# Attention and a softplus FFN on one core: the order tables of tiles 1 to 8, with GpSimd's block sums gathered between its maxima

## The chip, the cores and the metric

One core of a Trainium2 chip runs the whole program. The metric is device microseconds of one execution, as the median of 3 runs.

## The reference, cut to what matters

```python
q_s = softmax(q, axis=-1)            # max, exp, sum + 1e-9, divide; 64 values each
k_s = softmax(k, axis=2)             # over the 576 positions of a head
kv  = einsum('bhsd,bhse->bhde', k_s, v)
x   = einsum('bhsd,bhde->bhse', q_s, kv)   # 8 batches, 8 heads, 576 positions, 64 wide
x   = x.transpose(0, 2, 1, 3).reshape(4608, 512)
h   = x @ w_in                        # 512 x 2048
g   = maximum(h, 0) + log1p(exp(-abs(h)))
out = g @ w_out                       # 2048 x 512, float32
```

## The kernel before

The 4608 tokens are cut into 9 tiles of 512 (`SUBS`). The hidden width 2048 is cut into 16 chunks of 128. Float32 matrices are split into a high and a low part, so that one product costs three matmuls of 128x512. For each tile and chunk there is an up product (12 matmuls into a `ph` bank), ScalarE's softplus, a split into `g_hi` (ScalarE, L772) and `g_lo` (VectorE, L773), and two chunks later a down product (12 matmuls into the `po` banks).

Stage A is tile 0, ordered by the table `FIRST`. Stage B is tiles 1 and 2, ordered by `SINGLE`: 32 lines, one for each chunk. Line n says which steps are issued at three places, between bars: behind the up product of chunk n, behind its softplus, and behind the down product of chunk n-2. Within a line the split of chunk n-1 comes behind the first part. Stage C is tiles 3 to 8 in three pairs, ordered by the three lists of `PAIRS`. It uses fewer up products by working on sums and differences of `w_in` blocks and of token blocks. An engine executes its own instructions in the order in which they are issued, so these tables are the schedule; there is no planner at run time.

The steps in `SINGLE` prepare the next tiles. The first digit is the tile.

- `2u30` to `2u35` belong to one pair of heads of batch 2 (head pair 3): `0` the maximum of k over positions within a partition (VectorE, L418) and then across partitions (GpSimd's `partition_all_reduce`, L420, tile `mb`); `2` the subtraction of `mb` (VectorE, L435); `3` the exponential (ScalarE, L443); `4` the reciprocal of the sums (VectorE); `5` the split into `kv_hi` and `kv_lo` (ScalarE and VectorE in turn, L477 to L479). `2u3*` is the place at which the TensorE products of that unit stand (L448).
- `2q0` to `2q11` are the softmax of q: maxima of the two halves (`0`, `1`), exchange (`2`), subtraction (`3`, `4`, L573), exponential (`5`, `6`), sums (`7`, `8`, L579), inversion (`9`) and division (`10`, `11`).
- `2x00` to `2x33` are the product of q and kv: transposition (L661), split (L666, L668), TensorE's product at `2x0*` (L674), addition, and for tile 2 one more split.
- `p3` writes the w_in and w_out parts of chunk pair 3 to DRAM for stage C. `s30` to `s33` compute the sums of that pair's w_in blocks, mostly on GpSimd: `0` two additions (L974), `1` four additions of 128x256 (L977 to L980), `2` a copy on ScalarE (L984) and a subtraction on GpSimd (L985), `3` the stores by DMA (L990, L991).
- `f0` to `f10` prepare the sums of x for a pair, `U` and `D` load w for stage C, `2Q0` loads half a tile of q.

The sums need a place in SBUF, which is that of another tile that is dead by then; `SUM_SLOTS` lists them.

Of the kernel before, what the change touches and what calls it, by code (L numbers as in the profile page):

```python
# [44 lines left out]
SINGLE = [
    "||2u00",
    "2q0 2q1 2q2 2u10|p1 2u02 h0 2q4 2u12|",
    "2q6 s00 2q3 2u03 2u13|h1|2u0* 2u1* s01",
    "p0|2u14 2u20 2q5 2q8 2u22|2u30 2u04",
    "2u15||2u05",  # L50
    "s02 2u32 2u33 2u23 2q7 2q9 2q10|s10|2u2* 2d1 2u3*",
    "2u24 2u25 2x00 2d0|2u34 2x01 s11 2u35 3u00|",
    "2x0*|2x02 s12|s03",
    "2x03 2d2 s13 2x10 2x11||2q11 2x1* 2Q0 2x12 2d3 2x13",
    "2x20|2x21|",
    "2x2*||2x22 3u02",
    "2x23 2x30 3q0 2x31||3u10 2x3* 2x32 p2 3u12",
    "|2Q1 3q1|3u13 3q2",
    "p3 3q3 2x33 3q4 3u03 3u0* 3u1*|3u14 3u20 3u04 3q5 3q6|",
    "3u15|3q8 3u30 3u22 3u05 3q7 3u32|",  # L60
    "|3u23|3q9",
    "3u33|3u2* 3u3* 3q10 3u24|3u34 3u25",
    "3x00 3u35 3x01 4u00|4u10|3x0*",
    "s20 3x02 3x10 s21||p4 3x11 3q11",
    "s22 3x1* 3x12||3x20 3x21",
    "s23 s40||3x2*",
    "3x22|3x30 4u12 s41 s30|3Q0 p5",
    "3x31 s31 4u02 3Q1 s42|3x3* 4u13|",
    "4q0 3x32 s50 4q1 s43 4u03 s51 4u0* f0 4q2 s32|4u1* 4q3|4q4 s52 4u14",
    "s33 4u20|4q6 4u15 4q5|",  # L70
    "4u04 4u22 p7 s60 s53 4u30|p6 4u05 4u32 4q8 4q7 f1 4u33 s61 s70 4u23|",
    "||4q9 4u2* 4u3* 4u24 4q10 4u34 4u25 U0 U1 4x00 4u35 4x01 s71 4q11 s72",
    "||",
    "4x0* 4x02 4x10|4x11 s62|",
    "4x1* 4x12 s63 4x20||s73 4x21 f2",
    "4x2* 4x22 4x30|4x31|f4",
    "|4x3* 4Q1|4Q0 U2 4x32 D0 D1 D2",
]
PAIRS = [
    [  # L80
        "f5 f3 f6|S1.0 J1.0",
        "|f7 f10 S2.0",
        "f8 au00 f9 S3.0 J3.0|aq0 L1.0",
        "L4.0|au10 aq1 J2.0 g1.0",
        "|S1.1 au02 J1.1 aq2 au03",
        "g4.0 S2.1 au0* L1.1 aq3|L3.0 au12 au13",
        "aq4 S3.1|au04 J3.1",
        "aq6 aq8 J2.1 L4.1|",
        "g1.1|aq5 g4.1 S1.2 J1.2 au1*",
        "L2.0 S2.2 au20|",  # L90
        "au05 au14 S3.2 J3.2 aq7|",
        "au22 au30|au15 L1.2 L4.2 J2.2 g1.2",
        "au32 au23 S1.3|aq9 J1.3 au33 aq10",
        "g4.2 au2* au3* au34 au24 aq11 L1.3|L3.1 S2.3",
        "|au25 S3.3 J3.3 au35 ax00 g1.3 ax01",
        "bu00 L4.3|ax0* J2.3 ax02 ax10",
        "|aQ0 S1.4 J1.4 ax11",
        "ax1*|S2.4 g4.3",
        "L1.4 S3.4 bu10 bu12 J3.4 bq0|ax12 ax20 g1.4",
        "|L4.4 J2.4 ax21 L2.4",  # L100
        "S1.5 L2.1 ax2* J1.5|g4.4 bu02",
        "L1.5|L3.2 ax22 ax30 S2.5 ax31 aQ1 L3.4",
        "S3.5 J3.5|",
        "|g1.5 J2.5 bq1 L4.5 L2.2 bu03 bu13 bq2",
        "S1.6|ax3* J1.6 bq3",
        "ax32 bu0* bq4 bq5 S2.6 bq6 g4.5 L1.6 bu1*|bu14 L3.3",
        "S3.6 J3.6|bu04 L2.3 bq7",
        "J2.6 bu20 g1.6 L4.6|",
        "|bu30 S1.7 J1.7",
        "bq8 bu22 bu05 bu15 g4.6 bu32 S2.7|L1.7 bu23",  # L110
        "S3.7 bu33|bu2* L3.5 J3.7 bq9 bu3*",
        "|bu24 g1.7 bu25 L4.7 bq11 bq10 bu34 bx00 L2.5 J2.7 L2.6 g4.7",
        "bu35 bx01|",
        "G0|bx0*",
        "|",
        "G1 L2.7 bx02|G2 L3.6 bx10",
        "bx11|",
        "bx1* G3 G4|bQ0",
        "bx12 bx20|G5 bx21 L3.7",
        "|nf0 G6 bx2* nf1",  # L120
        "G7|nf2",
        "|bx22 bx30 G8",
        "|bx31 G9",
        "bx3* G10 bx32|",
        "|G11",
        "bQ1 nf4|nf10",
        "G12|",
        "nf5 G13 nf6 nf8|G14 nf3 nf9 G15 nf7",
    ],
    [  # L130
        "S1.0 J1.0|",
        "|S2.0 au00 L1.0",
        "au02 S3.0 au10|au12 J3.0",
        "L4.0|J2.0",
        "g1.0 aq1|S1.1 g4.0 J1.1 au13",
        "|S2.1 L3.0",
        "|aq0 S3.1 L1.1 au03 J3.1",
        "au0* au1*|J2.1 au04 aq2 L4.1 g1.1",
        "au14 au15 S1.2 aq4|J1.2 au05",
        "aq3 S2.2 L1.2|",  # L140
        "g4.1|aq5 au20 au30 S3.2 aq6 au22 J3.2",
        "aq7 au32 g1.2 J2.2|L4.2 au23",
        "S1.3 J1.3|g4.2",
        "S2.3 aq8 au33|",
        "au2* au3* au24|S3.3 L3.1 L3.2 J3.3 aq9 aq10 au34 L1.3 au25",
        "J2.3 ax00|L4.3 au35",
        "g1.3 ax01 S1.4 J1.4|ax0* ax02 g4.3 ax10",
        "bu00 S2.4|ax11 aq11 L1.4",
        "bu10|aQ0 S3.4 J3.4 L2.1 bu12 bu02 ax1* ax12",
        "L4.4|L2.3 J2.4",  # L150
        "ax20 g1.4 ax21 S1.5 bu13|J1.5 g4.4 ax2*",
        "L1.5|bq0 ax22 ax30 S2.5",
        "ax31 L2.4 S3.5|J3.5 bu03 g1.5 aQ1 L2.0 ax3* ax32 L3.5 bq1",
        "bu0*|J2.5 bu1* bq2 L4.5",
        "|bu20 bu04 bq4 bu22 bu30 g4.5 bu23 S1.6 bu14 bq6 J1.6",
        "L2.5 S2.6|L2.2",
        "S3.6 bu15 L3.3|J3.6 L1.6",
        "J2.6 bu32 L4.6 g1.6 bq3|",
        "L2.6|bq8 bu05 L3.4 S1.7 J1.7 g4.6",
        "|bq5 bu2* bq7 bu33 bq9 S2.7 bu3* bu34",  # L160
        "|bu24 bq10 bu25 bx00 S3.7 L1.7 bu35 J3.7",
        "g1.7 L4.7 bq11 J2.7|L3.7",
        "|bx01 g4.7",
        "bx0* G0 bx02|bx10",
        "|G1 G2",
        "|bx11",
        "G3 nf0|bx1*",
        "|G4",
        "bx12 G5|",
        "bx20 bx21 G6|",  # L170
        "bx2*|",
        "G7 bx22 bQ0|G8 bx30",
        "|nf2 L3.6",
        "bx31 G9 G10 bx3* nf4|",
        "bx32|G11",
# [7 lines left out]
        "L1.0 S3.0|J3.0",
        "g1.0 L4.0 J2.0|",
        "S1.1 g4.0 J1.1|",
        "L1.1 S2.1|L2.0",
        "|S3.1 J3.1",
        "|L4.1 g1.1 J2.1",
        "L3.0 S1.2 J1.2|g4.1",
        "|S2.2 L1.2",  # L190
        "S3.2 J3.2|",
        "J2.2 L4.2|L2.2 g1.2",
        "|S1.3 J1.3",
        "g4.2 S2.3 L1.3|",
        "S3.3 J3.3|g1.3",
        "L4.3 L2.1|J2.3",
        "S1.4 g4.3 L3.3 J1.4|",
        "|S2.4",
        "L3.2 L1.4|S3.4 J3.4",
        "|J2.4 L4.4",  # L200
        "g1.4|S1.5 J1.5 g4.4",
        "S2.5|",
        "S3.5|J3.5",
        "L1.5 J2.5|L4.5 g1.5",
        "S1.6 L3.1|L2.5 J1.6 L1.6 L3.4",
        "|g4.5 S2.6",
        "S3.6|J3.6",
        "|g1.6 L4.6 J2.6",
        "S1.7 J1.7|",
        "|S2.7 g4.6",  # L210
        "L1.7 L2.4 S3.7|J3.7",
        "|g1.7 J2.7 L4.7",
        "g4.7|",
        "G0 L3.6|",
        "|G1 L2.7 L2.6 L3.5 G2",
# [7 lines left out]
        "G8 G9|",
        "|G10",
        "G11|",
        "|G12",
        "|G13",
        "G14|",
# [1044 lines left out]
```

## Time and profile before

| | us |
|---|---|
| median of 3 runs | 892.82 (892.55 to 892.94) |
| the profiled execution | 891.69 |
| its span, first to last instruction | 889.9 |
| TensorE (PE) busy | 833.5 |
| VectorE (DVE) busy | 549.3 |
| ScalarE (ACT) busy | 520.4 |
| GpSimd (POOL) busy | 114.0 |

The span is covered by stage A from 0 to 119.67 us, stage B to 365.30 us and stage C to the end; the boundaries are the first up product of tile 1 and the first matmul of line 1118. Busy time of TensorE includes matmuls at half speed. A wait in brackets in a row names what ended it; "issue" means that the profile shows nothing that ended it. MODIFY_POOL_CONFIG is an instruction of GpSimd's sequencer, which the program's order shows as a bare "ISA" row.

### The profile page before, as it was taken

Reading aid. Unit: us, or ns where it says so; the run is one execution under the profiler, and the core shown is the slowest. Engines: PE = TensorE matmul, PEld = TensorE weight load, DVE = VectorE, ACT = ScalarE, POOL = GpSimd, SP = SyncE. Lnnn points to the kernel's source line nnn. Section 1 sums busy time; section 2 is a strip of 40 time slices with the busy share of each in tenths; the row PEclk is TensorE's granted clock in tenths of the full one; section 3 lists DMA queues with packets and bytes.
Section 4 is the critical chain, followed back from the end, with each engine's and each line's share of the span. In section 5 each row is a group of like instructions: output and inputs, shape, how many; then the busy total and the mean of one; then the engine's idle time right before and its main releaser. Section 6 shows DMA issues by size and latency. Waiting matters only on the chain.

```text
span 889.9 us, 11526 instructions
## 1 busy us (share of the span) xinstructions
PE 833.5 (94%) x4172; PEld 678.3 (76%) x4172; DVE 549.3 (62%) x849; ACT 520.4 (58%) x863; POOL 114.0 (13%) x203
## 2 busy tenths in 40 slices
...
PEclk9999999889989968999999999999999999999999
...
GB/s 341 376 346 54 26 149 141 101 140 174 78 171 198 275 117 114 277 203 211 233 232 231 245 215 201 218 247 179 202 211 236 190 177 244 164 218 156 142 222 108
DMA packets 79896, 172.72 MB, mean 194 GB/s; under 512 B 5088, under 2 KB 51936, under 8 KB 70624
## 3 DMA queue, kind: packets, MB, share of 16 engines
...
## 4 chain that ended last, share of the span: by engine, by line
PE 73%; DVE 8%; ACT 7%; issue 6%; POOL 3%; DMA 2%; SPq 0%; POOLq 0%; DVEq 0%; ACTq 0%
PE po L1138 28%; PE ph L1118 24%; PE po L795 3%; PE po L793 3%; PE po L794 3%; PE ph L758 3%; PE ph L760 3%; PE ph L759 3%; PE att L674 2%; PE att L448 1%; DMA kvt<-in_kv_tail 1%; DVE g_lo L773 1%; ACT g_hi L772 1%; POOL w L974 1%; PE po L791 1%
## 5 line engine op out<-in xcount | busy, mean ns | idle before, releaser
L1138 PE MATMUL po<-w,g_hi 128*128 128x512 f32 x784 | 246.0, 390 | 0.0
L1118 PE MATMUL ph<-w,w 128*128 128x512 f32 x864 | 213.0, 391 | 1.9 <-ACT w L1189 1.7
L1118 PEld LDWEIGHTS ph<-w,w 128*128 128x128 f32 x864 | 161.4, 188 | 36.8 <-ACT w L1189 2.1
L1138 PEld LDWEIGHTS po<-w,g_hi 128*128 128x128 f32 x784 | 146.8, 188 | 30.3
L1138 PE MATMUL po<-w,g_lo 128*128 128x512 f32 x392 | 153.1, 391 | 0.1
L1192 DVE TENSOR_TENSOR w<-ph,w 128x512 f32<-128x512 f32 x55 | 37.9, 689 | 99.1 <-PE ph L1118 54.5
L773 DVE TENSOR_TENSOR g_lo<-w,g_hi 128x512 fp32r<-128x512 f32 x74 | 51.0, 689 | 56.4 <-ACT g_hi L772 51.7
L1138 PEld LDWEIGHTS po<-w,g_lo 128*128 128x128 f32 x392 | 73.6, 188 | 15.8 <-DVE g_lo L773 0.5
L793 PE MATMUL po<-w,g_hi 128*128 128x512 f32 x164 | 68.5, 418 | 12.1 <-ACT g_hi L772 12.1
L772 ACT CAST g_hi<-w 128x512 fp32r<-128x512 f32 x74 | 45.8, 619 | 55.5 <-PE po L1138 55.1
L795 PE MATMUL po<-w,g_lo 128*128 128x512 f32 x164 | 68.3, 416 | 4.7 <-DVE g_lo L773 4.6
L1189 ACT COPY w<-ph 128x512 f32<-128x512 f32 x55 | 32.1, 584 | 67.2 <-PE ph L1118 67.0
L794 PE MATMUL po<-w,g_hi 128*128 128x512 f32 x164 | 67.7, 413 | 0.0
L420 POOL PARTITION_ALL_REDUCE mb<-mx x28 | 25.4, 906 | 270.7 <-DVE mx L418 231.1
L758 PE MATMUL ph<-x,w 128*128 128x512 f32 x142 | 58.0, 408 | 0.0
L759 PE MATMUL ph<-x,w 128*128 128x512 f32 x142 | 56.3, 397 | 0.0
L760 PE MATMUL ph<-x,w 128*128 128x512 f32 x142 | 56.0, 394 | 0.0
L668 DVE TENSOR_TENSOR two<-att,two 64x512 fp32r<-64x512 f32 x56 | 38.6, 689 | 20.1 <-ACT two L666 19.6
L793 PEld LDWEIGHTS po<-w,g_hi 128*128 128x128 f32 x164 | 32.9, 200 | 19.7 <-ACT g_hi L772 13.2
L773 DVE TENSOR_TENSOR g_lo<-l,g_hi 128x512 fp32r<-128x512 f32 x46 | 37.8, 822 | 11.6 <-ACT g_hi L772 11.0
L666 ACT CAST two<-att 64x512 fp32r<-64x512 f32 x56 | 32.5, 580 | 19.9 <-DVE att L661 19.2
L795 PEld LDWEIGHTS po<-w,g_lo 128*128 128x128 f32 x164 | 33.0, 201 | 14.6 <-DVE g_lo L773 7.4
...
## 6 DMA issues: line engine op xcount, KB each, us to landing
...
```

The costliest lines, as they stand in the source:

```text
L668: nc.vector.tensor_tensor(out=w[SIDE[1 - z], z], in0=ps[zs], in1=w[zs, z].bitcast(F32), op=ALU.subtract)
L758: nc.tensor.matmul(ph, lhsT=w_hi, rhs=x_hi, start=h == 0, stop=False)
L759: nc.tensor.matmul(ph, lhsT=w_lo, rhs=x_hi, start=False, stop=False)
L760: nc.tensor.matmul(ph, lhsT=w_hi, rhs=x_lo, start=False, stop=h == HP - 1)
L772: copy(g_hi, l)
L773: nc.vector.tensor_tensor(out=g_lo, in0=l, in1=g_hi.bitcast(F32), op=ALU.subtract)
L793: nc.tensor.matmul(po, lhsT=g_hi[:, ms], rhs=w_hi, start=j == chunks(t)[0], stop=False)
L794: nc.tensor.matmul(po, lhsT=g_hi[:, ms], rhs=w_lo, start=False, stop=False)
L795: nc.tensor.matmul(po, lhsT=g_lo[:, ms], rhs=w_hi, start=False, stop=j == chunks(t)[-1])
L1118: nc.tensor.matmul(bank, lhsT=a, rhs=b, start=start and e == k == 0, stop=e == 1 and k == 2, skip_group_check=True)
L1138: nc.tensor.matmul(po, lhsT=g[:, cs], rhs=w, start=first and k == 0, stop=end and k == 2)
L1192: nc.vector.tensor_tensor(out=l[k, p], in0=ph_b, in1=l[k, p], op=ALU.add)
```

## The change

The contents of `SINGLE` and `PAIRS` are written anew, with the same steps, and `SUM_SLOTS` gives other places for six of the eight sums. `FIRST` and all functions are as before.

```diff
 SINGLE = [
-    "||2u00",
-    "2q0 2q1 2q2 2u10|p1 2u02 h0 2q4 2u12|",
...
-    "4q0 3x32 s50 4q1 s43 4u03 s51 4u0* f0 4q2 s32|4u1* 4q3|4q4 s52 4u14",
+    "|2u00 2q1 2u10 2u02|",
+    "|2u12 2u03 p1 2q0 2q2 h0 2u13 2q4|",
...
+    "s42 3x21|3x2*|s32 3x22 3x30 s43 s52 3Q1 3x31",
+    "4q1||",
+    "3x3* 4u00|3x32 4u10 p5 4u02|4u12 4u03",
+    "4u13 4u0* 4q0|4u1*|",
+    "s53 p6 4q2 4u04 4q3 4q4 4u20 4u14 4u30 4u22 4q5 4q6|4u32 s33 s60 4u05 4q7 4u33|4q8 4u15 4u23 4q9",
+    "||4u2* 4u24 4u3* 4q10 4u34 U0 4u25",
...
-SUM_SLOTS = "x2", "w1", "x1", "x1", "w3", "w4", "w5", "w6"
+SUM_SLOTS = "x2", "w1", "x0", "x1", "spare", "w2", "w3", "w4"
```

On GpSimd the kernel before has, around the units 0 and 1 of batch 4 (`mb` is the result of the maxima, the `w_` names are parts and sums of w_in, and a bare ISA is MODIFY_POOL_CONFIG):

```order
L985 TENSOR_TENSOR w_2488<-w_2488 128x1024
L420 ISA
L420 ISA mb<-mx 128x128
L974 ISA
L974 TENSOR_TENSOR w_2639<-w_1002 128x512
L974 TENSOR_TENSOR w_2639<-w_1098 128x512
L420 ISA
L420 ISA mb<-mx 128x128
L977 ISA
L977 TENSOR_TENSOR w_2639<-w_2639 128x256
L978 TENSOR_TENSOR w_2639<-w_2639 128x256
L979 TENSOR_TENSOR w_2639<-w_2639 128x256
```

At the same units the changed kernel has (`x_2289`, `spare` and `w_2321` are the sums of the pairs 3, 4 and 5):

```order
L979 TENSOR_TENSOR w_2321<-w_2321 128x256
L980 TENSOR_TENSOR w_2321<-w_2321 128x256
L985 TENSOR_TENSOR spare<-spare 128x1024
L985 TENSOR_TENSOR x_2289<-x_2289 128x1024
L985 TENSOR_TENSOR w_2321<-w_2321 128x1024
L420 ISA
L420 ISA mb<-mx 128x128 x2
L371 MEMSET kvt 64x2x64
```

The two maxima stand behind one another, with one bare ISA row ahead of them instead of one ahead of each and one ahead of each sum. In tiles 1 and 2 and up to the first maximum of stage C there are 12 such rows before and 6 after.

On VectorE the kernel before has, in line 25 of `SINGLE` (tile 4's q and k, two lines into its softmax), between two splits of g:

```order
L773 TENSOR_TENSOR g_lo_1959<-l_1877,g_hi_1958 128x512
L458 TENSOR_SCALAR r_1964<-att1_108 128x1
L459 RECIPROCAL r_1964<-r_1964 128x1
L418 TENSOR_REDUCE mx_1967<-kvt_1936 128x128
L458 TENSOR_SCALAR r_1971<-att0_107 128x1
L459 RECIPROCAL r_1971<-r_1971 128x1
L479 SCALAR_TENSOR_TENSOR kv_hi11_96<-att1_108,r_1964,kv_hi11_96 64x64
L479 SCALAR_TENSOR_TENSOR kv_lo11_104<-att1_108,r_1964,kv_lo11_104 64x64
L773 TENSOR_TENSOR g_lo_2007<-l_1962,g_hi_2006 128x512
```

At the same units the changed kernel has between two splits of g:

```order
L773 TENSOR_TENSOR g_lo_1972<-l_1879,g_hi_1971 128x512
L573 TENSOR_TENSOR q0_1846<-q0_1846,m_1872 128x1024
L479 SCALAR_TENSOR_TENSOR kv_hi11_96<-att1_108,r_1956,kv_hi11_96 64x64
L479 SCALAR_TENSOR_TENSOR kv_lo11_104<-att1_108,r_1956,kv_lo11_104 64x64
L418 TENSOR_REDUCE mx_1997<-kvt_1934 128x128
L418 TENSOR_REDUCE mx_2002<-kvt_1950 128x128
L435 TENSOR_TENSOR kvt_1950<-kvt_1950,mb_2004 128x10x64
L773 TENSOR_TENSOR g_lo_2020<-l_1975,g_hi_2019 128x512
```

A subtraction of q, both maxima of units 2 and 3 and the subtraction of unit 2 now stand ahead of that split; before there was one maximum.

## Rows read from the trace of the kernel before

**Rows 1.** The page: busy time of each engine; TensorE's granted clock in 40 slices.

```profile
PE 833.5 (94%) x4172; PEld 678.3 (76%) x4172; DVE 549.3 (62%) x849; ACT 520.4 (58%) x863; POOL 114.0 (13%) x203
...
PEclk9999999889989968999999999999999999999999
```

**Rows 2.** Busy time by window, stages B and C: length, engines, clock, DMA.

```profile
119.67:365.30 245.63, 208.14 (x1057) 167.42 (x1056) 159.59 (x239) 138.94 (x233) 88.73 (x120) 0.91 0.46 153
365.31:890.00 524.69, 516.36 (x2481) 424.38 (x2479) 281.63 (x426) 283.11 (x467) 14.88 (x42) 1.00 0.59 207
```

**Rows 3.** TensorE's timeline in stage B: start, duration, line, operands.

```profile
119.67 0.39 PE L758 MATMUL ph<-x,spare 128*128 128x512 f32 x1
...
125.11 0.39 PE L758 MATMUL ph<-x,w 128*128 128x512 f32 x1
...
175.49 0.30 PE L674 MATMUL att<-two,kv_hi 128*128 128x128 f32 x1 [2.52 <-DVE two L668]
...
178.20 0.63 PE L794 MATMUL po<-w,g_hi 128*128 128x512 f32 x1
178.63 0.63 PE L795 MATMUL po<-w,g_lo 128*128 128x512 f32 x1
...
188.32 0.22 PE L674 MATMUL att<-two,kv_hi 128*128 128x128 f32 x1
...
188.89 0.39 PE L758 MATMUL ph<-x,w 128*128 128x512 f32 x1
...
282.61 1.39 PE L448 MATMUL att<-kvt 128*64 128x65 f32 x40
```

**Rows 4.** What TensorE waited for, 120 to 366 us: total, times, longest.

```profile
PE att L448 <- issue: 16.1, 2, 13.8
PE po L793 <- ACT g_hi L772: 12.1, 3, 4.6
PE po L795 <- DVE g_lo L773: 4.6, 3, 1.8
```

**Rows 5.** The chain of work that ended last, 296 to 345 us.

```profile
298.88 4.04 issue
...
303.73 7.38 issue
...
313.82 5.81 issue
...
320.44 6.64 issue
```

**Rows 6.** GpSimd's sequencer at line 420, 191 to 210 us: durations (ns), starts.

```profile
L420 POOLq MODIFY_POOL_CONFIG  x2: 4/4/4, 193.0 to 193.0; - x2
```

**Rows 7.** GpSimd's timeline in stage B.

```profile
207.20 0.72 POOL L420 PARTITION_ALL_REDUCE mb<-mx  x1 [14.40 <-DVE mx L418]
...
311.11 2.47 POOL L974 TENSOR_TENSOR w<-w 128x512 f32<-128x512 f32 x2 [7.46 <-issue]
...
339.40 2.36 POOL L985 TENSOR_TENSOR w<-w 128x1024 fp32r<-128x1024 f32 x1 [1.16 <-ACT w L984]
```

**Rows 8.** VectorE's timeline in stage B.

```profile
339.88 2.43 DVE L773 TENSOR_TENSOR g_lo<-l,g_hi 128x512 fp32r<-128x512 f32 x1 [3.57 <-ACT g_hi L772]
...
344.54 0.69 DVE L773 TENSOR_TENSOR g_lo<-l,g_hi 128x512 fp32r<-128x512 f32 x1
```

**Rows 9.** VectorE by line and form, 119.67 to 365.3 us: busy, mean ns, idle before.

```profile
L773 DVE TENSOR_TENSOR g_lo<-l,g_hi 128x512 fp32r<-128x512 f32 x32 | 28.1, 880 | 10.1 <-ACT g_hi L772 9.8
L418 DVE TENSOR_REDUCE mx<-kvt 128x128 f32<-128x640 f32 x12 | 15.8, 1315 | 5.9 <-DMA kvt<-in_kv_tail 4.6 <-POOL x L978 1.2
L435 DVE TENSOR_TENSOR kvt<-kvt,mb 128x640 f32<-128x640 f32 x12 | 10.3, 858 | 24.0 <-POOL mb L420 23.9
L573 DVE TENSOR_TENSOR q<-q,m 128x1024 f32<-128x1024 f32 x6 | 10.0, 1675 | 0.0
L579 DVE TENSOR_REDUCE s<-q 128x32 f32<-128x1024 f32 x6 | 7.2, 1208 | 0.0
```

More of the change, by code (lines that the diff above doesn't have):

```diff
@@ L45 @@
 SINGLE = [
-    "||2u00",
-    "2q0 2q1 2q2 2u10|p1 2u02 h0 2q4 2u12|",
[L48 to L68, printed above, removed]
-    "4q0 3x32 s50 4q1 s43 4u03 s51 4u0* f0 4q2 s32|4u1* 4q3|4q4 s52 4u14",
-    "s33 4u20|4q6 4u15 4q5|",
-    "4u04 4u22 p7 s60 s53 4u30|p6 4u05 4u32 4q8 4q7 f1 4u33 s61 s70 4u23|",
-    "||4q9 4u2* 4u3* 4u24 4q10 4u34 4u25 U0 U1 4x00 4u35 4x01 s71 4q11 s72",
@@ L73 @@
-    "||",
[L74 to L77, printed above, removed]
+    "|2u00 2q1 2u10 2u02|",
+    "|2u12 2u03 p1 2q0 2q2 h0 2u13 2q4|",
+    "2u0* 2q6 2q3 2q8 2u1*|h1|2u20",
+    "|2u04 2u30 2u14 2u05 2u15|",
+    "s00 p0 2u22 2u32||2q5 2u33",
+    "2q7 2q9 2u23|2u2* 2d0 2u24 2u3* 2q10|2u25 2x00",
+    "|s01 2q11|2d1 2u34 2x01 2u35 s02",
+    "s03 2d2 2x0* 2x02||2x03 2d3 2x10 2x11 s10",
+    "||2x1*",
+    "2x12|s11 2x13 s12 p3|s13",
@@ new lines @@
+    "2x20 2x21 2x2* 2x22|2x23|2x30",
+    "3u00 3u10 2x31||3u12 2Q0",
+    "2Q1 3u02 2x3* 2x32 3q1||2x33",
+    "3q0 3q2 p2 3u03 3u13 3u0* 3u1* 3u14 3q4 3u04 p4|3q3 3u15|3q5 3u20 3q6 3u30 3u32",
+    "||",
+    "3q8 3q7 s20 3u22|3u05 3q9 3u33 3q10 3u23|",
+    "3u2* 3u24 3u3*||",
+    "3u25 s21 3u34 3x00 3x01|s22 3q11|",
+    "3u35|3x0* s23 3x02 3x10|3x11 3Q0",
+    "s30 s40 s31||3x1* s50 p7 3x12",
+    "3x20 s41||s51",
+    "s42 3x21|3x2*|s32 3x22 3x30 s43 s52 3Q1 3x31",
+    "4q1||",
+    "3x3* 4u00|3x32 4u10 p5 4u02|4u12 4u03",
@@ L78 @@
+    "4u13 4u0* 4q0|4u1*|",
+    "s53 p6 4q2 4u04 4q3 4q4 4u20 4u14 4u30 4u22 4q5 4q6|4u32 s33 s60 4u05 4q7 4u33|4q8 4u15 4u23 4q9",
+    "||4u2* 4u24 4u3* 4q10 4u34 U0 4u25",
+    "4x00|4u35|4x01",
+    "4x0* f1 4x02 s70 4x10|s71|",
+    "U1 4x11 s72 4q11 4x1* 4x12 4x20||4x21 s61 f0",
+    "4x2*||s73 4x22 4x30 s62",
+    "s63 4x31|U2 D1 4x3*|4Q0 4Q1 f2 4x32 D0 D2 f4",
 ]
@@ L80 @@
     [
[L81 to L114, printed above, removed]
-        "|",
[L116 to L128, printed above, removed]
-    ],
-    [
[L131 to L175, printed above, removed]
-        "|",
-        "L2.7 nf1 G12|nf3 nf5 G13 nf7 nf6 nf8 bQ1 G14",
-        "nf10|nf9 G15",
@@ new lines @@
+        "f5 f3 f6 S1.0 J1.0|",
+        "|f8 f7 f10 S2.0",
+        "au00 f9 S3.0|J3.0",
+        "au02 L1.0 J2.0 au10 L4.0 g1.0|aq1 au12",
+        "|au03 S1.1 J1.1",
+        "|S2.1 au13",
+        "L1.1 aq0 au0* aq2 aq4 S3.1 g4.0 au1*|J3.1",
+        "|g1.1 aq6 L4.1 L3.0 au14 J2.1",
+        "aq3|g4.1 S1.2 J1.2 aq5 au20",
+        "|S2.2 L1.2",
+        "au30|au22 S3.2 J3.2",
+        "aq7|aq8 au15 aq9 J2.2 L4.2",
+        "au04 L3.1 au32 g1.2 g4.2 S1.3 au05 J1.3|",
+        "au23 aq10 au2* S2.3 au33 au3* aq11 au24 au34|L1.3 au25 L2.1",
@@ new lines @@
+        "S3.3 ax00 J3.3|",
+        "ax01 au35 g1.3|J2.3 L4.3 ax0* bu00",
+        "ax02 S1.4 ax10|J1.4",
+        "|L1.4 aQ0 g4.3 ax11 S2.4 ax1*",
+        "ax12|S3.4 J3.4 ax20 g1.4",
+        "J2.4 bq0 ax21 L4.4|bu10",
+        "S1.5 J1.5|ax2* L2.0 ax22",
+        "L2.2 ax30 g4.4 S2.5 bu02|aQ1",
+        "|ax31 S3.5 J3.5 L1.5 ax3* L2.4",
+        "bu12 bq1 bq2 bu13 J2.5 L4.5|g1.5 L3.4 bq4 ax32",
+        "bu03|S1.6 bu0* g4.5 J1.6 bu1*",
+        "bq6|S2.6",
+        "bu20 L2.3 bq3 L3.2 bu04|S3.6 L1.6 bu14 J3.6",
@@ new lines @@
+        "J2.6|L4.6 g1.6",
+        "bq8 S1.7 bu22 bu30|bu23 J1.7 bu32 bq5",
+        "|S2.7 bq7 g4.6 bq9",
+        "bu05 bu15 bu33|bu2* S3.7 bu24 J3.7 bq10 bu3*",
+        "L1.7 g1.7 bu25 bq11 L3.7 bx00 L4.7 bu34 J2.7|L2.5",
+        "g4.7 bx01|G0 bu35",
+        "|G1",
+        "bx0*|bx02",
+        "G2 bx10 L3.6|",
+        "nf1|bx11 L3.3 G3 bx1*",
+        "G4 nf0|",
+        "bx12 bx20 G5|",
+        "bx21|bx2*",
+        "nf2 L2.6 L2.7 G6 G7 bx22 L3.5|G8 bx30 bx31",
+        "|",
+        "G9|",
```

144 lines of the change are left out of this document (99 added, 45 removed).

## The prediction, made before the change was run

> **What bounds the kernel now.** First the page's busy times and its row of the granted clock [rows 1]: TensorE is busy for 94% of the span, and the clock falls below 9 tenths in one region only, the slices from about 155 to 356 us. That region is stage B. The windows by stage say the same in numbers [rows 2]: in stage B TensorE is busy for 208.14 of 245.63 us at a mean granted clock of 0.91; in stage C for 516.36 of 524.69 at 1.00. So idle time is 37.5 us in B and 8.3 in C.
>
> How much of B is loss? A line of the table is 24 matmuls, and at full clock one takes 125.11 - 119.67 = 5.44 us [rows 3]. 32 lines are 174.1 us. Twelve kv units come in six pairs of 1.39 us (8.3), and twelve x products take 188.89 - 188.32 = 0.57 each (6.8) [rows 3]. Together 189.2 us, against 245.6: 56.4 us are lost in B, 37.5 of them idle. Most of the other 19 are matmuls at half speed: behind the gap of 2.52 us they start every 0.43 us (178.20, 178.63) instead of 0.227 [rows 3], which is 1.2 instead of 2.4 GHz.
>
> What TensorE waits for is read next [rows 4]: 16.1 us for kv products (one wait of 13.8), 12.1 for g_hi, 4.6 for g_lo. None of these is slow work. The chain names the cause [rows 5]: between 298 and 328 us it holds four pieces of "issue", 4.04, 7.38, 5.81 and 6.64, which lie alternately ahead of a maximum and ahead of a sum on GpSimd. Each time GpSimd goes from sums to `partition_all_reduce` or back there is a MODIFY_POOL_CONFIG, and then 6 to 7.5 us in which it does nothing [rows 6, 7]: 7.46 from the maximum of 303.6 to the addition of 311.11. VectorE stands at the subtraction of `mb` meanwhile, 23.9 us in all [rows 9], and it issues in order: g_lo and the kv splits behind it are late too.
>
> One more reading decides what a switch costs elsewhere. Before the maximum at 207.20 GpSimd had been idle for 14.40 us, yet it started as soon as VectorE's maximum was there [rows 7]; the switch had begun at 193.0, right behind the last sum [rows 6]. A switch therefore runs ahead of its data, and it is free if about 7 us lie between the last operation of one kind and the first need of the other.
>
> By the Trainium skill (GPSIMD Engine Reference, Instruction dispatch) the first call into freshly loaded code pays about 6 us. The trace agrees for the maxima and shows up to 1.5 us more for the sums.
>
> **The change part by part.** *Switches.* 12 become 6. I went through the six that stay.
> - Lines 4, 15 and 25, into sums (`s00`, `s20`, `s60`): the maxima of all four units are done, so only ScalarE's copies `s02`, `s22`, `s62` need the result, and these stand two to five lines later. 7.5 us and two additions (2.47) and four small ones (3 us) are 13; two lines are 11 us, and for `s22` the switch can start behind the maximum in line 13. No cost.
> - Line 11, into maxima (`3u00`): `s12` is in line 9. No cost; the same for the first maximum of stage C.
> - Line 23, into maxima (`4u00`): three subtractions of 2.4 us stand in lines 21 and 22, then 6 us. By this count the result is there when line 23 is 6 us old, about when VectorE reaches `4u02`. With what VectorE has ahead of it, `4u0*` waits about 1 us.
>
> So the issue pieces of the chain go (the four of [rows 5] are 23.9 us), and with them the backlog that each left on VectorE and ScalarE. What is late next is VectorE's own load.
>
> *Dense lines.* I summed the work by line. Ahead of the exponential `4u23` line 25 has two L573 of 1.68, two maxima of 1.32, two L435 of 0.86, two L579 of 1.21 [rows 9], together 10.1 us, one g_lo of 0.69, and some 20 short operations that I estimate at 3.8: 14.6 us, and about 1.4 for turns with ScalarE. VectorE begins it some 2.4 us ahead of TensorE's line, so `4u23` is through 13.6 us into the line; TensorE arrives at `4u2*` after two lines, 10.9 us. That is a new wait of 2.7 us. Lines 13 to 15 are alike (VectorE 11.0, 0.7 and 7.6 us against 6.8, 5.4 and 5.4), and the same count gives 2.6 us at `3u2*`. Lines 5, 8 and 23/24 give 0.5, 0.5 and 1.0. Sum 7.3 us. Two of these waits are long enough to bring the half clock, as the wait of 2.52 us did [rows 3]; 12 matmuls (one down product) at 0.2 us extra make 2.4 each, 4.8 together. So far 12.1.
>
> *GpSimd beside VectorE.* g_lo took 2.43 us while a subtraction ran on GpSimd (339.40 to 341.76) and 0.69 alone [rows 7, 8]. Eight such subtractions stay. From below the burst costs nothing (lines 19, 20 and 22 have only 2 us of VectorE each); from above each holds one g_lo that TensorE waits for, 8 times 1.74, 14 us. I take half, 7 us, since in the kernel before, too, only some of the slow ones show as waits (4.6 us for g_lo [rows 4]).
>
> The Trainium skill (SBUF — State Buffer, Summary: rules for kernel authors) says that of a VectorE operation with two SBUF inputs and a GpSimd operation the second to issue fully blocks. The trace agrees at 339.88. By the rule alone the burst would hold every such operation in lines 19 to 23; the rival C below prices it.
>
> *Stage C.* Its tables are new as well, with the same steps and the same matmuls. Its idle time is 8.3 us [rows 2], and part of that is the end, which no table moves. So it can hardly gain more than 4 us; `f2` and `f4` now stand at the end of B, which puts about 1 us ahead of the first pair. I take 0, with 4 us gained and 6 lost as ends. *SUM_SLOTS:* each new place is free when it is asked for (the latest is `w2`, free behind the down product of line 19, where `s50` stands); it costs nothing unless the stores come later than in line 18 (`3x02` waits for those of `s23`, hidden by about one line).
>
> Sum: B loses 12 + 7 = 19 instead of 56.4, a gain of 37.4. The profiled execution of 891.69 becomes 854.3; the median is 1.1 above that execution, so 855.4, which I round to 855.
>
> **The rivals.**
> A. The dense lines cost their whole overhang. Lines 13, 15, 25 and 29 have 4.2, 2.1, 9.7 and 2.4 us more VectorE than TensorE; if nothing catches up, 18.4 us and four stretches at half speed (9.6), with 7 for the port and 2 elsewhere make 37 lost, a gain of 19: 873. For it: VectorE is at 15 us in one line of 5.4. Against it: the next lines are nearly empty, and lines of 10 us stood in the table before without waits of their own.
> B. Only the four pieces on the chain go, 23.9 us, and other waits take the place of the backlog: 891.7 - 23.9 + 1.1 = 869. For it: the chain holds them whole. Against it: half the loss of B is neither of them, but the half clock and the late splits that follow.
> C. The burst blocks VectorE. If all eight subtractions hold up TensorE and three of the gaps bring the half clock, 14 + 7 instead of 7: 869. For it: 339.88. Against it: VectorE has little to do there.
> D. Slower. Stage C's new order makes TensorE wait: 96 places in the two pairs that carry attention, and from 0.4 us for each of them (38 us) the gain is gone; at 0.5, 48 us, the time is 903. For it: every row there changed. Against it: there the work on VectorE and ScalarE is 54% of the length each, and TensorE's whole idle time is 8.3 us [rows 2].
> E. The switches are fewer but were hidden anyway: no change. Against it stands the wait of 13.8 us directly behind them [rows 4, 5].
>
> **How the numbers follow.** Forecast 0.60, 843 to 866; A 0.14; B 0.09; C 0.07; D 0.06; E 0.04. The range of 8 in 10 takes in A, B and C, and below it the case that B loses 4 us only and stage C gains 3: 892.8 - 52 - 3 = 838. I give 839 to 881. About 0.2% is what the measurement tells from no change. Faster is the first four, 0.90; within 0.2% 0.04; slower 0.06.
>
> **What would show it.** Right: 6 switches in stage B; no "issue" ahead of the subtraction L435 and no wait of more than 3 us at kv products; the window of B near 208 us with a granted clock of 0.96 or more; C within 5 us of 524.7. The first waits to look for are at `3u2*` and `4u2*`, under 3 us each, with VectorE busy through them. Wrong: a MODIFY_POOL_CONFIG on the chain again, matmuls at half speed over more than two stretches, or C longer by over 10 us.

## The result, and the profile after

The changed kernel takes 854.23 us (median of 4 runs, 853.95 to 854.53), the kernel before on the same chip 892.72; the ratio is 0.957, with a 95% interval of 0.955 to 0.959. The forecast was 855.0. The profiled execution took 854.46 us, with a span of 852.7.

The page of the changed kernel, busy time of each engine and TensorE's granted clock in 40 slices:

```profile
PE 823.4 (97%) x4172; PEld 673.4 (79%) x4172; DVE 543.0 (64%) x849; ACT 519.1 (61%) x861; POOL 115.8 (14%) x203
...
PEclk9999999999999999999999999999999999999999
```

The slices in which the clock lay below 9 tenths [rows 1] are gone. TensorE's busy time fell by 10.1 us with the same 4172 matmuls: fewer of them ran at half speed.

The windows of the changed kernel, stages B and C: length, busy time of PE, PEld, DVE, ACT and POOL, granted clock, DMA share, GB/s:

```profile
119.61:328.55 208.94, 196.87 (x1057) 160.69 (x1056) 152.28 (x239) 136.53 (x231) 88.20 (x120) 0.98 0.53 173
328.56:852.70 524.14, 516.44 (x2481) 424.33 (x2479) 282.92 (x427) 284.35 (x467) 17.15 (x42) 1.00 0.59 209
```

Beside [rows 2], stage B is 36.7 us shorter and stage C 0.6. In B, TensorE's idle time went from 37.5 to 12.1 us and its busy time from 208.1 to 196.9. GpSimd's busy time in B did not change (88.7 and 88.2): its work is the same, and what went are its pauses.

What TensorE waited for in stage B (total, times, longest), and VectorE's wait for `mb`:

```profile
PE att L674 <- DVE two L668: 5.0, 5, 1.9
PE att L448 <- issue: 3.0, 1, 3.0
PE att L674 <- DVE kv_lo L479: 1.7, 2, 1.0
PE att L448 <- ACT kvt L443: 1.2, 2, 1.0
PE att L448 <- POOL x L974: 1.1, 1, 1.1
```

```profile
DVE kvt L435 <- POOL mb L420: 2.0, 3, 0.8
```

Of [rows 4], the wait of 13.8 us is gone, as are the 12.1 for `g_hi` and the 4.6 for `g_lo`. The subtraction of `mb` waited 23.9 us before [rows 9] and waits 2.0 now.

GpSimd's sequencer from 119 to 366 us, with two rows for each switch (times in ns, then first and last start):

```profile
L420 POOLq MODIFY_POOL_CONFIG  x6: 12/18/28, 187.2 to 324.1; - x6
L974 POOLq MODIFY_POOL_CONFIG  x6: 87/88/88, 145.2 to 286.8; - x6
```

and four places of GpSimd's own timeline:

```profile
194.21 0.73 POOL L420 PARTITION_ALL_REDUCE mb<-mx  x1 [7.21 <-DVE mx L418]
...
222.66 2.50 POOL L974 TENSOR_TENSOR x<-w 128x512 f32<-128x512 f32 x2 [6.91 <-DVE kv_lo L479]
...
270.28 0.72 POOL L420 PARTITION_ALL_REDUCE mb<-mx  x1 [6.74 <-issue]
...
294.42 3.70 POOL L974 TENSOR_TENSOR w<-w 128x512 f32<-128x512 f32 x2 [7.58 <-DVE s L584]
```

Three switches toward each side, 6 instead of 12. The first maximum waited for VectorE's `mx`, not for its switch, which had begun at 187.2. Only at 270.28 (line 23) does the profile name nothing that ended the pause, and TensorE's gap behind it, at `4u1*`, is 0.28 us. The pauses ahead of the two sums are as long as a switch as well, whatever the profile names there, but the sums are for stage C, and TensorE waits for none of them here. The 1.1 us that the list above puts on a sum end at 224.57, when ScalarE's exponential for that product has just ended (224.47). In the kernel before, eight pauses of GpSimd in stage B are put down to "issue", 53.1 us in all; here it is this one.

### The profile page after: what moved, and what is told of

Its sections match the earlier page's. It is cut to its first block, busy times and chain, and to the rows that moved or that the text cites. A ratio compares the mean times of both kernels' runs of the same rounds, so it can differ in the third digit from the quotient of the medians.

```text
span 852.7 us, 11505 instructions
## 1 busy us (share of the span) xinstructions
PE 823.4 (97%) x4172; PEld 673.4 (79%) x4172; DVE 543.0 (64%) x849; ACT 519.1 (61%) x861; POOL 115.8 (14%) x203
## 4 chain that ended last, share of the span: by engine, by line
PE 75%; DVE 9%; ACT 7%; issue 4%; DMA 3%; POOL 2%; SPq 0%; DVEq 0%; ACTq 0%; POOLq 0%
PE po L1138 29%; PE ph L1118 24%; PE ph L758 3%; PE ph L759 3%; PE ph L760 3%; PE po L793 3%; PE po L795 3%; PE po L794 3%; DMA kvt<-in_kv_tail 2%; PE att L674 2%; PE att L448 1%; DVE q L587 1%; DVE g_lo L773 1%; DVE two L668 1%; ACT two L666 1%
## 5 line engine op out<-in xcount | busy, mean ns | idle before, releaser
L1138 PE MATMUL po<-w,g_hi 128*128 128x512 f32 x784 | 246.0, 390 | 0.0
L1138 PEld LDWEIGHTS po<-w,g_hi 128*128 128x128 f32 x784 | 146.7, 188 | 30.4
L1138 PE MATMUL po<-w,g_lo 128*128 128x512 f32 x392 | 152.8, 390 | 0.5 <-DVE g_lo L773 0.5
L773 DVE TENSOR_TENSOR g_lo<-w,g_hi 128x512 fp32r<-128x512 f32 x77 | 52.8, 690 | 56.3 <-ACT g_hi L772 52.5
L1138 PEld LDWEIGHTS po<-w,g_lo 128*128 128x128 f32 x392 | 73.6, 188 | 16.3 <-DVE g_lo L773 0.9
L793 PE MATMUL po<-w,g_hi 128*128 128x512 f32 x164 | 65.3, 398 | 0.0
L795 PE MATMUL po<-w,g_lo 128*128 128x512 f32 x164 | 64.9, 396 | 0.0
L794 PE MATMUL po<-w,g_hi 128*128 128x512 f32 x164 | 64.9, 396 | 0.0
L420 POOL PARTITION_ALL_REDUCE mb<-mx x28 | 28.1, 1003 | 256.5 <-DVE mx L418 236.8
L758 PE MATMUL ph<-x,w 128*128 128x512 f32 x142 | 56.9, 400 | 0.0
L759 PE MATMUL ph<-x,w 128*128 128x512 f32 x142 | 55.5, 391 | 0.0
L760 PE MATMUL ph<-x,w 128*128 128x512 f32 x142 | 55.4, 390 | 0.0
L418 DVE TENSOR_REDUCE mx<-kvt 128x128 f32<-128x640 f32 x28 | 36.9, 1329 | 9.9 <-DMA kvt<-in_kv_tail 9.8
L766 ACT ACTIVATE l<-ph 128x512 f32<-128x512 f32 (+1 forms) x50 | 29.1, 581 | 14.9 <-PE ph L760 13.6
L773 DVE TENSOR_TENSOR g_lo<-l,g_hi 128x512 fp32r<-128x512 f32 x46 | 34.1, 741 | 4.8 <-ACT g_hi L772 4.0
```

The costliest lines, as they stand in the source:

```text
L758: nc.tensor.matmul(ph, lhsT=w_hi, rhs=x_hi, start=h == 0, stop=False)
L759: nc.tensor.matmul(ph, lhsT=w_lo, rhs=x_hi, start=False, stop=False)
L760: nc.tensor.matmul(ph, lhsT=w_hi, rhs=x_lo, start=False, stop=h == HP - 1)
L773: nc.vector.tensor_tensor(out=g_lo, in0=l, in1=g_hi.bitcast(F32), op=ALU.subtract)
L793: nc.tensor.matmul(po, lhsT=g_hi[:, ms], rhs=w_hi, start=j == chunks(t)[0], stop=False)
L794: nc.tensor.matmul(po, lhsT=g_hi[:, ms], rhs=w_lo, start=False, stop=False)
```

## The experiments

Ratios are to the kernel before on the same chip, with their 95% interval. B is the length of stage B in the profile.

**1. Only the new tables of stage C**: the kernel before with the new `PAIRS`.

```diff
-        "f5 f3 f6|S1.0 J1.0",
-        "|f7 f10 S2.0",
...
+        "f5 f3 f6 S1.0 J1.0|",
+        "|f8 f7 f10 S2.0",
...
```

> The kernel before with the new tables of stage C alone. Theory (the gain is in stage B, by the switches of GpSimd that went): 889 to 895 us, stage B 243 to 248 us, stage C 522 to 527. Rival (the new tables of stage C gain by themselves or need the old ones to lose): below 885 or above 898 us.

Measured: 891.06 us, 0.9991 [0.9982, 1.0000].

**2. Only the new table of stage B**: the changed kernel's `SINGLE` and `SUM_SLOTS` with the old `PAIRS` (the cut shows the changed kernel against this run).

```diff
-        "f5 f3 f6 S1.0 J1.0|",
-        "|f8 f7 f10 S2.0",
...
+        "f5 f3 f6|S1.0 J1.0",
+        "|f7 f10 S2.0",
...
```

> The new table of tiles 1 and 2 and the new places of the sums, with the old tables of stage C. Theory: 851 to 858 us, all of the gain, stage B 207 to 211 us. Rival (part of the gain needs the new stage C): above 862 us.

Measured: 856.45 us, 0.9607 [0.9592, 0.9621]; B 209.2 us. So the gain is stage B's. Between this run and the changed kernel lie 0.38% (3 us) by the medians; the two profiles differ by 1.6 us, of which 0.7 are in stage C.

**3 and 4. No switches and short sums, in either order.** Each addition or subtraction of the sums became a copy of one input. A copy needs no MODIFY_POOL_CONFIG: up to the first maximum of stage C there is none left.

```diff
-    add(out=y, in0=hi, in1=lo, op=ALU.add)
+    nc.gpsimd.tensor_copy(out=y, in_=lo)
...
-    add(out=lo.bitcast(F32R), in0=lo, in1=hi, op=ALU.subtract)
+    nc.gpsimd.tensor_copy(out=lo.bitcast(F32R), in_=hi)
```

> The kernel before, in its own order, with GpSimd copying one input where it adds or subtracts two (the sums' values are left out); a copy needs no switch, so all 12 switches of stage B go and nothing is moved. Theory (the switches in the path cost the 37 us): 848 to 862 us, no wait over 3 us in stage B. Rival (the new layout of the attention steps gains, with or without switches): 875 to 892 us.

> The changed kernel with the same copies (the sums' values are left out), so without any switch in stage B and with shorter work on GpSimd. Theory (the six switches left are hidden, and GpSimd beside VectorE costs up to 7 us): 847 to 854 us. Rival (a switch costs its 6 to 7.5 us wherever it stands): 810 to 820 us.

Measured: the old order 846.84 us, 0.9499 [0.9485, 0.9514]; the new one 847.77, 0.9506 [0.9490, 0.9523]. Stage B of the two, old order first:

```profile
119.79:319.18 199.39, 193.33 (x1057) 158.35 (x1056) 149.07 (x239) 139.19 (x233) 54.26 (x120) 0.99 0.57 188
```

```profile
119.75:322.04 202.29, 192.71 (x1057) 156.96 (x1056) 144.79 (x239) 136.31 (x231) 53.22 (x120) 1.00 0.55 181
```

Run 3 came out just below its forecast (848 to 862), run 4 inside. Without switches the old order is as good as the new one. The rival, that the layout of the attention steps gains by itself, falls. But a copy takes half as long as an addition (0.79 us for 128x512 against 1.52 in the old order), so two things were taken away at once; runs 9 to 12 part them.

**5. A switch put back into the path**: the changed kernel with one addition of 128x4 elements between the two maxima of line 23.

```diff
-    "3x3* 4u00|3x32 4u10 p5 4u02|4u12 4u03",
+    "3x3* 4u00 Z|3x32 4u10 p5 4u02|4u12 4u03",
```

> The changed kernel with one addition of 128x4 on GpSimd between the maxima of 4u00 and 4u10 in line 23, which brings two more switches between two maxima that VectorE waits for. Theory: 13 us on GpSimd, of which TensorE sees 8 to 14, and one stretch at half speed: 862 to 870 us. Rival (only the number of operations and their order on VectorE matters): 853 to 856 us.

Measured: 864.38 us, 0.9693 [0.9672, 0.9713]. GpSimd's timeline, and TensorE's at the kv product of unit 1, whose maximum stands behind the addition:

```profile
278.40 0.19 POOL L1045 TENSOR_TENSOR small<-small 128x4 f32<-128x4 f32 x1 [7.05 <-issue]
284.74 0.72 POOL L420 PARTITION_ALL_REDUCE mb<-mx  x1 [6.16 <-issue]
```

```profile
287.16 1.35 PE L448 MATMUL att<-kvt 128*64 128x65 f32 x20 [11.54 <-ACT kvt L443]
```

An operation of 0.19 us with a switch on either side held TensorE for 11.54 us, where the gap was 0.28. Both pauses (7.05 and 6.16) are "issue", as in [rows 5].

**6. As many switches where nothing waits**: three such additions in the first pair of stage C, so that there are 12 switches again.

```diff
-        "|S2.1 au13",
+        "|S2.1 au13 Z",
...
-        "au04 L3.1 au32 g1.2 g4.2 S1.3 au05 J1.3|",
+        "au04 L3.1 au32 g1.2 g4.2 S1.3 au05 J1.3| Z",
...
-        "L2.2 ax30 g4.4 S2.5 bu02|aQ1",
+        "L2.2 ax30 g4.4 S2.5 bu02|aQ1 Z",
```

> The changed kernel with three such additions in the first pair of stage C, each between two groups of maxima over 15 us apart: 12 switches in all, as before the change. Theory (a switch runs ahead of its data and is free there): 853 to 857 us. Rival (each switch costs 6 to 7.5 us): 888 to 899 us.

Measured: 856.65 us, 0.9605 [0.9584, 0.9625]. Stage C, where the switches were added, took 524.33 us (524.14 without), so they cost nothing there. The 0.36% beside the changed kernel lie for the most part ahead of them: its stage B began 1.4 us later and took 0.6 us more, which I can't explain from the trace. So two more switches cost 10 us in run 5, and six more nothing that can be seen where they stand: the place decides.

**7 and 8. The dense lines.** In run 7 two subtractions of q left line 25 for the end of line 24; in run 8 also a division of q left line 6 for line 8.

```diff
-    "4u13 4u0* 4q0|4u1*|",
-    "s53 p6 4q2 4u04 4q3 4q4 4u20 ...
+    "4u13 4u0* 4q0|4u1* 4q2 4q3|",
+    "s53 p6 4u04 4q4 4u20 ...
```

```diff
-    "|s01 2q11|2d1 2u34 2x01 2u35 s02",
+    "|s01|2d1 2u34 2x01 2u35 s02",
...
-    "||2x1*"
+    "||2x1* 2q11"
```

> The changed kernel with 4q2 and 4q3 moved from line 25 to the end of line 24, 3 us of VectorE earlier. Theory (the wait of 2.98 us at 4u2* is the load of VectorE in line 25): the wait falls under 1.5 us, 851 to 853 us. Rival (the wait comes from the DMA of the kv tail, which the maximum of 4u30 waited for): 854 to 855 us.

> The same, and 2q11 moved from line 6 to the end of line 8, which takes 1.7 us of VectorE out of the way of 2x0* in line 7. Theory (VectorE's order makes the 2.3 us of waits there, and these the only stretch at half speed): 846 to 850 us, no stretch at half speed in line 7. Rival (ScalarE's copies of stack_kv are what is late): 851 to 854 us.

Measured: 854.65 us, 0.9586 [0.9570, 0.9602], and 853.91 us, 0.9583 [0.9560, 0.9606]. Both expectations missed; neither differs from the changed kernel. Run 7 did not do what it was meant to: its two subtractions (L573) begin at 277.37 instead of 278.06, because nothing but two short operations stood between the old place and the new one on VectorE. VectorE's two maxima of units 2 and 3 in run 7, TensorE's `4u2*` in run 7 and, last, in run 10 (below):

```profile
280.39 1.37 DVE L418 TENSOR_REDUCE mx<-kvt 128x128 f32<-128x640 f32 x1 [0.29 <-DMA kvt<-in_kv_tail]
...
282.76 1.35 DVE L418 TENSOR_REDUCE mx<-kvt 128x128 f32<-128x640 f32 x1 [0.73 <-DMA kvt<-in_kv_tail]
```

```profile
292.27 1.39 PE L448 MATMUL att<-kvt 128*64 128x65 f32 x40 [2.54 <-issue]
```

```profile
288.07 2.44 PE L448 MATMUL att<-kvt 128*64 128x65 f32 x40 [2.54 <-issue]
```

Both maxima wait for the DMA of k's tail. From the start of the second maximum to `4u2*` it is 9.51 us here and 9.52 in the changed kernel (283.58 to 293.10); in the other profiles of the new order with this stretch (runs 2, 4, 6, 8, 10 and 11) it is 9.0 to 9.5. In all eight one maximum or both wait for k's tail (0.26 to 1.64 us). So by the traces this wait hangs on when k's tail lands and on what stands behind that maximum on VectorE and ScalarE; no run changed either of them by itself. The wait is 2.42 and 2.29 us in runs 2 and 6, which leave line 25 alone, 2.54 in run 7 and 1.72 in run 8. The same wait of 2.54 us is followed by a kv product at full speed in run 7 (1.39) and at half speed in run 10 (2.44): its length alone does not decide the clock. In run 8 the wait at `2x0*` shrank from 2.30 us in two pieces to 1.00, and `2x1*` one line later took it over (TensorE at `2x1*`, then ScalarE):

```profile
177.85 0.31 PE L674 MATMUL att<-two,kv_hi 128*128 128x128 f32 x1 [2.50 <-DVE two L668]
```

```profile
172.68 0.59 ACT L710 CAST x<-att 128x512 fp32r<-128x512 f32 x1 [2.45 <-DMA low<-x]
```

The second row shows ScalarE held by the store of the first sum out of slot `x2`. Whether that alone holds `2x1*` was not tried.

**9 and 12. Length and switches apart, old order.** Run 9 has the copies of run 3 and one addition of 128x4 elements ahead of each group of a sum: short work, all 12 switches. Run 12 makes each copy twice: work as long as before, no switch.

```diff
+    nc.gpsimd.tensor_tensor(out=small[:, 0:4], in0=small[:, 4:8], in1=small[:, 4:8], op=ALU.add)
     nc.gpsimd.tensor_copy(out=y, in_=lo)
```

```diff
-    nc.gpsimd.tensor_copy(out=y, in_=lo)
+    for _ in range(2):
+        nc.gpsimd.tensor_copy(out=y, in_=lo)
```

> The kernel before with one-input copies on GpSimd in place of the additions and subtractions of the sums (the values of the sums are left out), as in the earlier run that took 846.8 us and has no switch, and with one addition of 128x4 elements (0.19 us) ahead of each of the sums' groups, which brings the 12 switches back at their places. GpSimd's own work stays as short as in that run. Theory (the switches that stand in the path cost the 38 us, not the length of the sums or the port): 872 to 892 us, window of stage B 224 to 244 us, waits for GpSimd at the subtraction of mb of over 15 us. Rival (the length of the additions beside VectorE is what cost): 846 to 855 us, window of B under 207 us.

> The kernel before with each addition or subtraction of the sums replaced by the same copy of one input made twice (the values of the sums are left out). GpSimd is then busy with the sums about as long as before (two copies of 0.79 us for an addition of 1.52, two of 1.15 for a subtraction of 2.48) but has no switch. With the kernel before (890: long sums, switches), the run with copies (847: short, none) and the one with copies and short additions (865: short, switches) it is the fourth corner. Theory (length costs 25 us in the kernel before only because a switch starts when the sums ahead of it are done; without switches it costs what it does in the changed kernel, some 6 us): 848 to 857 us. Rival (length by itself, GpSimd beside VectorE, costs the 25 us in this order): 868 to 875 us.

Measured: 864.71 us, 0.9713 [0.9693, 0.9733], and 856.71 us, 0.9609 [0.9591, 0.9627]. Stage B of run 9 and of run 12:

```profile
119.82:337.85 218.03, 199.84 (x1057) 162.56 (x1056) 147.66 (x239) 138.94 (x233) 57.59 (x144) 0.95 0.52 172
```

```profile
119.78:331.84 212.06, 200.19 (x1057) 162.68 (x1056) 154.47 (x239) 138.91 (x233) 92.40 (x176) 0.96 0.54 177
```

| stage B, old order | no switch | 12 switches |
|---|---|---|
| short sums | 199.4 | 218.0 |
| long sums | 212.1 | 245.6 |

The switches alone cost 18.6 us, the length alone 12.7, and both together 46.2: 15 us belong to neither. Each entry is one profile, and that of run 12 is its slowest execution (858.14); by the ratios of the medians the three parts are 19.1, 9.8 and 15.8 us. The expectation for run 9 missed in time and in stage B, because it put all of the 38 us on the switches at any length; VectorE's wait for `mb`, 15.8 us, was as expected. That for run 12 came out at its upper end: length alone costs 9.8 us, not "some 6". What is late in run 9 is the same kind of place as before; TensorE at a kv product:

```profile
302.69 2.44 PE L448 MATMUL att<-kvt 128*64 128x65 f32 x40 [9.98 <-issue]
```

A likely reading of the 15 us is that GpSimd works in order: a switch toward the maxima starts when the sums ahead of it are done, so longer sums push it out of what hid it. Nearly all of the 15 is idle time of TensorE and not the clock: by the windows TensorE idles for 6.1 us without either, 18.2 in run 9, 11.9 in run 12 and 37.5 with both, which leaves 13.5 that belong to neither. The reading itself has no run of its own.

A copy reads one input where an addition reads two, so run 12 may also spare VectorE something. By the traces that is little: the splits g_lo still take 814 ns in run 12, against 880 before, and VectorE is busy for 154.5 us of stage B against 159.6. I estimate from this that at most some 5 us of the difference between the two can have this cause.

**10 and 11. The same in the new order.** Run 10 is run 4 with the additions of 128x4 elements (short work, 6 switches). Run 11 is the changed kernel with only the eight subtractions of L985 as copies.

```diff
-    add(out=lo.bitcast(F32R), in0=lo, in1=hi, op=ALU.subtract)
+    nc.gpsimd.tensor_copy(out=lo.bitcast(F32R), in_=hi)
```

> The changed kernel with the same copies (the values of the sums are left out) and the same additions of 128x4 elements ahead of each group, so that its 6 switches are there and GpSimd's work is short. The same kernel without the additions took 847.8 us, the changed kernel itself 854.2. Theory (the six switches are hidden, and the 6.4 us between the two are the length of the sums and the port shared with VectorE): 847 to 850 us, window of B 202 to 204 us. Rival (the 6.4 us are the switches that are left): 852 to 855 us, window of B 207 to 209 us.

> The changed kernel with copies of one input in place of the eight subtractions of 128x1024 elements at L985 alone (the lower halves of the sums' operands are left out); the additions and their 6 switches stay. Each takes about 1.2 us instead of 2.4. Theory of the prediction (GpSimd's long subtractions hold up VectorE's splits g_lo, and these cost 7 us, half of it or more by their length): 848 to 851 us. Rival (they stand in lines where VectorE has little to do, and cost nothing): 853 to 855 us.

Measured: 847.40 us, 0.9520 [0.9499, 0.9541], and 851.10 us, 0.9554 [0.9536, 0.9572]. Stage B of run 10 and of run 11:

```profile
119.79:322.09 202.30, 193.51 (x1057) 158.46 (x1056) 144.69 (x239) 136.42 (x231) 55.99 (x144) 0.99 0.55 181
```

```profile
119.74:324.73 204.99, 195.60 (x1057) 159.44 (x1056) 148.34 (x239) 136.41 (x231) 76.47 (x120) 0.98 0.55 179
```

B is 202.3 us with six switches and 202.3 without any (run 4), and the ratios, 0.9520 and 0.9506, can't be told apart: in the new order the switches cost nothing that can be measured. With the full sums B is 208.9, so their length costs 6.6 us by the profiles (4.4 by the ratios of the changed kernel and run 10), and run 11 puts 3.9 of these on the eight subtractions. Run 11 lies a tenth of a microsecond above its theory's range, and by its ratio it can't be told from the changed kernel (the intervals of 0.9554 and 0.9569 overlap); the 3.9 rests on one profile of each.

No version that computes the reference is faster than the changed kernel by more than the intervals.

## Why the prediction was right, point by point

*What bounded the kernel.* Right: the gain is in stage B, and its cause is the switches. The old order at about the old length, without switches, has 0.9609 (run 12) against 0.9569 for the change: 34.9 us of the 38.5 come back when the switches go and nothing is moved; up to some 5 of these may be due to the copies' single input. Run 12 takes all 12 away at once, so it does not tell what each cost. The change gains 3.6 us more (the two intervals do not quite touch), and with the sums short the new layout gains nothing (runs 3 and 4).

*The loss of B.* Forecast 19 us, measured 208.9 - 189.2 = 19.7. That this is so close is in part luck. The measured loss is 12.1 us of idle time, some 4.2 at half speed, and some 3.5 by which the count of 189.2 is too low: in run 4, where no matmul of 128x512 is at half speed, TensorE is busy for 192.71 us. The forecast had 7.3 + 7 = 14.3 us of waits and 4.8 at half speed, and its count made up the rest. Of the 56.4 us before, "most of the other 19 are matmuls at half speed" holds, but not by much: in the trace of before I find six stretches with 54 matmuls of 128x512 at half speed, 10.8 us at 0.2 each, and two kv products that took 1.5 us longer together.

*The six switches that stay.* Right: no cost in the lines called free (runs 4 and 10). In line 23 I gave 1 us at `4u0*`; there is no gap there, and 0.28 us at `4u1*`.

*Dense lines, 7.3 us of new waits.* Near in size at the places named (5.3 us), at `4u2*` by chance, and half wrong in place. TensorE's timeline of the changed kernel at the largest gaps, in lines 7 and 26:

```profile
166.02 0.30 PE L674 MATMUL att<-two,kv_hi 128*128 128x128 f32 x1 [1.30 <-DVE two L668]
167.32 0.45 PE L674 MATMUL att<-two,kv_lo 128*128 128x128 f32 x1 [1.00 <-DVE kv_lo L479]
...
168.31 0.63 PE L793 MATMUL po<-w,g_hi 128*128 128x512 f32 x1
168.74 0.63 PE L794 MATMUL po<-w,g_hi 128*128 128x512 f32 x1
...
293.10 2.44 PE L448 MATMUL att<-kvt 128*64 128x65 f32 x40 [2.98 <-issue]
295.47 0.80 PE L758 MATMUL ph<-x,w 128*128 128x512 f32 x1
```

`4u2*` waits 2.98 us where 2.7 were forecast. `3u2*` waits 1.07 instead of 2.6, line 5 0.97 instead of 0.5, line 8 not at all; with line 23/24 that makes 5.3 us at the places named. (The loads given for lines 13 to 15 sum to 19.3 against 17.6 us, which is 1.7 and not yet the 2.6 forecast for `3u2*`.) Another 6.5 us stand where the count had nothing: 2.30 in line 7 (the wait that stood there before, 2.52 and 1.00), 0.70, 1.02, 1.91 and 0.58 in lines 18, 21, 30 and 31. VectorE in line 25 shows what the count left out at `4u2*`:

```profile
278.06 2.34 DVE L573 TENSOR_TENSOR q<-q,m 128x1024 f32<-128x1024 f32 x2
280.32 1.36 DVE L418 TENSOR_REDUCE mx<-kvt 128x128 f32<-128x640 f32 x1
...
283.58 1.35 DVE L418 TENSOR_REDUCE mx<-kvt 128x128 f32<-128x640 f32 x1 [1.64 <-DMA kvt<-in_kv_tail]
...
288.90 2.35 DVE L579 TENSOR_REDUCE s<-q 128x32 f32<-128x1024 f32 x2
```

The two L573 took 1.2 us each instead of 1.68, and VectorE then stood for 1.64 us until k's tail had landed. So VectorE was not busy all through this wait, as the forecast had it: the DMA sets when the second maximum starts, and the work behind it, 9.5 us to the product, does the rest (run 7). The 2.7 came out because what was over in one term was missing in the other.

*Half speed, 4.8 us in two stretches.* Right in number and size. Measured: two, some 4.2 us. One is behind the gaps of line 7, 13 matmuls that start every 0.43 us (2.6 us). The other is behind `4u2*`, where the kv product takes 2.44 us instead of 1.39 [rows 3] and the first up products start 0.59 and 0.41 apart (1.6 us together). The place of the first was not the one forecast (`3u2*`). That a wait of some 2.5 us brings the half clock, as the forecast took it, does not hold in every run: behind `4u2*` it came in run 10 and not in run 7.

*GpSimd beside VectorE, 7 us (0 to 14).* Right in size, 6.6 us by run 10, and wrong in its path. The forecast had splits g_lo that TensorE waits for; in stage B of the changed kernel TensorE's list has no wait for g_lo. What shrinks in run 10 are the waits for the x products (L674), from 5.0 + 1.7 us to 2.8 + 0.7 (the rows of run 10):

```profile
PE att L674 <- DVE two L668: 2.8, 4, 1.5
PE att L674 <- DVE kv_lo L479: 0.7, 1, 0.7
```

That is 3.2 of the 6.6 us. The other 3.4 are busy time (196.87 against 193.51), for the most part the stretch at half speed in line 7, which run 10 does not have and which the forecast counted in another term. The splits of B by form, in the changed kernel:

```profile
L773 DVE TENSOR_TENSOR g_lo<-l,g_hi 128x512 fp32r<-128x512 f32 x32 | 24.4, 763 | 4.0 <-ACT g_hi L772 3.6
```

The mean is 763 ns against 880 before [rows 9] and 696 in run 10, so over 32 splits the sums' length costs VectorE 2.1 us here. A split by itself takes 690. By the Trainium skill (SBUF — State Buffer, Summary: rules for kernel authors), of a VectorE operation with two SBUF inputs and a GpSimd operation that reads SBUF, the second to issue fully blocks. The traces agree at the one place that the prediction shows (2.43 us at 339.88), and most other splits lose far less. They show that the length of the sums costs time in either order; that the port is what does it, rather than the later maxima, no run here parts.

*Stage C.* Forecast 0 (-4 to +6). Measured -0.6 us in the profile, and run 1 gives 0.9991.

*The rivals.* A (873): TensorE's idle time in B is 12.1 us in all, where A has 18.4 for the overhang alone. B (869): the backlog behind the four pieces went with them; the longest wait that took their place is the 2.98 us at `4u2*`. C (869): the eight subtractions cost 3.9 us in run 11, not 14. D (903) falls by run 1, E by the result and by run 5. What the forecast did not see is that length and switches together cost more than the two apart: it priced them as separate terms. In the new order this does no harm, because the six switches are hidden and the length alone is left.
